# RWKV-7 recurrence and SiLU feed-forward in one kernel: the feed-forward of chunks 0 and 1 worked one chunk at a time, with 256 columns

## The chip, the core and the metric

The kernel runs on one core of one Trainium2 chip. The metric is the time on the device in microseconds, from a launch of the whole program; several runs are taken and the median is given. A profile is one further execution under the hardware profiler; its span reaches from the first to the last instruction of the program.

## What is computed

Two blocks follow each other. The first is a linear recurrence for 4 batches and 8 heads with head dimension 40 over 768 tokens, in float32:

```
for t in range(S):
    y[t]  = r[t] @ state                      # state: D x D per batch and head
    Sa    = state @ a[t]
    state = state * w[t][None, :] - outer(Sa, b[t]) + outer(v[t], k[t])
```

Its output, as 3072 tokens of 8 x 40 = 320 features, goes through a feed-forward block:

```
h = x @ w_in                    # 320 -> 2048
g = h * (1 / (1 + exp(-h)))     # SiLU
out = g @ w_out                 # 2048 -> 320
```

The weights w_in and w_out arrive as float64. The kernel sees them as pairs of 32-bit words and turns them into float32 itself.

## The kernel before

**Chunks and units.** The 768 tokens are cut into 12 chunks of 64 (`NN` = 12). In every chunk there are two units (`NM` = 2), each of two batches. Within a chunk the recurrence is written with matrices: token-by-token products, a triangular system, and a carried state. `pre(u)` prepares a unit before its turn: `scale` (L251 to L262) scans the decays w into running products W on VectorE (L253), takes their reciprocals (L255, VectorE), scales a and kb on GpSimd (L256, L258) and keeps a check on ScalarE (L261, L262); `scores` multiplies b with a on TensorE (`pm`, L231), masks on VectorE (L239) and sends the result to DRAM (`md`, L274). It also asks for the next unit's w (L219), which goes into the one tile `w` that all units from chunk 2 on share. `inverse` then inverts the triangular blocks of two chunks at once, row by row on VectorE (L310, L316), in 15 rows for chunks 0 to 3 and 31 rows from chunk 4 on; `merge` joins the blocks on TensorE (L357, L371, L380 for the 16-row form, L407 and L424 for both).

**The chain.** `chain(u, xs)` is what one unit does in its turn: `keys` (transposes, L473), `right` (L231, L483, L495), `solve` (`pu` L517, `pw` L535), `read` (`pl` L571, masked into `vl` at L579), `write` (`pgy`, L593 and L603; the state Gbd is updated by L616 and L620, and the outputs `yx` of L625 are stored to `xs` in DRAM by L631), and `turn` (L555), which transposes the state for the next chunk. A chunk needs the state that the one before left, so the chains follow one another.

**The feed-forward.** `moe(c, xs)` serves two chunks together: 512 token columns. `fetch` reads `xs` back as `xt` (L646, L648). Then come 16 steps: four `first` (each 256 hidden features: six matmuls `ph`, L658 and L663, of 512 columns; a sigmoid on ScalarE, L666, and the product on VectorE, L667, into `gts`), four `second` (each 128 tokens: eight accumulating matmuls `po`, L674, of 320 columns), and the same again for the other half of the hidden features, where the four `second` add up both halves and store to `out`. The three PSUM banks of `moe_bank` are shared by `ph` and `po`. `in_order` ties every feed-forward matmul behind the one before.

**The weights.** `load_weights(n)` and `weights(n)` bring in 40 pieces, 20 for each half of the hidden features: ten of w_in, then ten of w_out. A piece takes five VectorE instructions (L164, L165, L173, L175, L176) and three on ScalarE (L166 to L168). Raw pieces lie in rooms: up to piece `NG` = 24 four of five lie in a tile that shares its place with `gts`, and pieces from 24 on use the three places `room`, `mi` and `tmp` in rotation. The pieces are asked for five ahead at first, three ahead later.

**Order.** `weave` mixes lists of steps by their relative places. A scheduler then puts the instructions of each engine into one fixed order, and may move a later step forward where it finds the engine free; every engine works off its order strictly. The DMAs go through SyncE's queue in the same manner (some early ones through ScalarE's). The lists for chunks 0 to 3 before the change:

```
weave(steps, convert[6:19])                       # chunk 0's chain
weave(steps[0:4], convert[19:21])                 # chunk 1's chain
weave(steps[4:], convert[21:26], prepare(2))
fetch, queue = moe(0, xs); fetch()
weave(queue[0:12], prepare(3) + convert[26:] + invert(3))
```

From then on the remaining feed-forward steps form a queue, of which chunks 2 and 3 take none by name, and every later chunk takes eight (`now`); what is left at the end is run last.

Of the kernel before, what the change touches and what calls it, by code (L numbers as in the profile page):

```python
# [9 lines left out]
F32 = mybir.dt.float32  # L10
I32 = mybir.dt.int32
U32 = mybir.dt.uint32
AF = mybir.ActivationFunctionType
ALU = mybir.AluOpType
# [18 lines left out]
def weave(*lists):  # L33

    at = [(i + 0.5) / len(x) for x in lists for i in range(len(x))]
    steps = [s for x in lists for s in x]
    for i in sorted(range(len(steps)), key=lambda i: at[i]):
        steps[i]()
# [3 lines left out]
def kernel(  # L42
# [15 lines left out]
    nc = tc.nc  # L58
    NM, NN = aT.shape[0] // 2, aT.shape[1]
# [15 lines left out]
    def moe_bank(name):  # L75
        return ps.tile([128, 512], F32, name=name, tag="moe", bufs=3)
# [52 lines left out]
    for half in range(2):  # L129
# [5 lines left out]
                pieces.append((wl_f[:, c // 2 : c // 2 + WS], [(64 * n, 64 * n + 64, odd[:, n]) for n in range(2)]))  # L135
        for c in range(NF * DM // 2 * half, NF * DM // 2 * (half + 1), WS):
            pieces.append((wo_f[:, c : c + WS], [(0, 128, w_out[:, 2 * c : 2 * (c + WS)])]))
    NW, NG = len(pieces), 24
    rooms = {}

    def load_weights(n, queue=nc.sync):

        if n == 0:
            rooms["gts"] = sb.tile([128, 4, 4 * WS], I32, name="room4", tag="gts")
        if n < NG and n % 5 < 4:
            rooms[n] = rooms["gts"][:, n % 5]
        else:
            tag = "room" if n < NG else ("room", "mi", "tmp")[n % 3]
            rooms[n] = sb.tile([128, 4 * WS], I32, name="room", tag=tag)
        for lo, hi, src in pieces[n][1]:  # L150
            raw = rooms[n][lo:hi, 0 : 2 * WS]
            queue.dma_start(raw.rearrange("p (i x) -> p i x", x=256) if len(src.shape) == 3 else raw, src)
# [46 lines left out]
    def load(u):  # L199
        u.a = sb.tile([128, Q, C], F32, name="a", bufs=4)  # L200
        u.kb = sb.tile([128, Q, 2, C], F32, name="kb", bufs=6)
        B2 = slice(2 * u.m, 2 * u.m + 2)

        def part(n, x):
            for be in range(2):
                nc.sync.dma_start(
                    u.kb[:, P * be : P * be + P, n], x[2 * u.m + be, u.n].rearrange("p (q t) -> p q t", q=P)
                )

        nc.sync.dma_start(  # L210
            u.a.rearrange("p (b q) t -> p b (q t)", b=2), aT[B2, u.n].rearrange("b p c -> p b c")
        )
        part(1, bT)
        part(0, kT)
# [247 lines left out]
    def chain(u, xs):  # L462
# [13 lines left out]
        def right():  # L476
            u.sk = sb.tile([128, 2, P, C], F32, name="sk", bufs=2)
            between(u, 0, u.sk)
            pr = [bank("pr") for _ in range(2)]

            for p in range(P if u.n > 0 else 0):
                for be in range(2):
                    nc.tensor.matmul(  # L483
                        pr[be][C * be : C * be + C, p * 80 : p * 80 + 80],
                        lhsT=u.a[:, P * be + p, :],
                        rhs=gbd[:, P * be + p],
                        start=p == 0,
                        stop=False,
                        skip_group_check=True,
                    )  # L490
            for p in range(P):
                for j in range(2):
                    for be in range(2):
                        R = slice(C * be, C * be + C)
                        nc.tensor.matmul(  # L495
                            pr[be][R, p * 80 + j * D : p * 80 + j * D + D],
                            lhsT=u.sk[R, j, p, :],
                            rhs=u.v2[R, 2 * p + j, :],
                            start=u.n == 0 and p == 0 and j == 0,
                            stop=True,  # L500
                            skip_group_check=True,
                        )
            for be in range(2):
                R = slice(C * be, C * be + C)
                nc.scalar.copy(
                    out=rhs[R, :, :, 0:D],
                    in_=pr[be][R, 0 : H * D].rearrange("p (q j d) -> p q j d", q=P, j=2),
                )
# [127 lines left out]
        return [keys, right, solve, read, write] + ([] if last else [turn])  # L636


    def moe(c, xs):
        T = 4 * NM * C  # L640
        box = {}
        ots = [None] * (T // 128)

        def fetch():
            xt = box["xt"] = sb.tile([128, 3, T], F32, name="xt")
            nc.sync.dma_start(xt[:, 0:2], xs[0:256].rearrange("(k r) t -> r k t", k=2))  # L646
            for n in range(2):
                nc.sync.dma_start(xt[64 * n : 64 * n + 64, 2], xs[256:DM])  # L648

        def first(i):  # L650
            if i % (NF // 4) == 0:
                box["gts"] = sb.tile([128, NF // 2, T], F32, name="gts")
            xt = box["xt"]
            ph = [moe_bank("ph") for _ in range(2)]
            for n in range(2):
                for k in range(2):
                    at = (2 * i + n) * 128
                    in_order(nc.tensor.matmul(  # L658
                        ph[n], lhsT=wi_s[:, k, at : at + 128], rhs=xt[:, k, :], start=k == 0, stop=False
                    ))  # L660
            for n in range(2):
                R = slice(64 * n, 64 * n + 64)
                in_order(nc.tensor.matmul(ph[n], lhsT=wl_s[R, i, :], rhs=xt[R, 2, :], start=False, stop=True))  # L663
            for n in range(2):
                sg = sb.tile([128, T], F32, name="sg", bufs=2)
                nc.scalar.activation(out=sg, in_=ph[n], func=AF.Sigmoid)  # L666
                nc.vector.tensor_tensor(  # L667
                    out=box["gts"][:, (2 * i + n) % (NF // 2), :], in0=ph[n], in1=sg, op=ALU.mult
                )

        def second(half, b):
            po = moe_bank("po")
            for f in range(NF // 2):
                in_order(nc.tensor.matmul(  # L674
                    po[:, 0:DM],
                    lhsT=box["gts"][:, f, b * 128 : b * 128 + 128],
                    rhs=wo_s[:, NF // 2 * half + f, :],
                    start=f == 0,
                    stop=f == NF // 2 - 1,
                ))  # L680
            if half == 0:
                ots[b] = sb.tile([128, DM], F32, name=f"ot{b}")
                nc.scalar.copy(out=ots[b], in_=po[:, 0:DM])
                return
            ot = ots[b]
            nc.vector.tensor_tensor(out=ot, in0=po[:, 0:DM], in1=ot, op=ALU.add)
            n, m = 2 * c + b // NM, b % NM
            for be in range(2):
                at = (2 * m + be) * S + C * n
                nc.sync.dma_start(out[at : at + C, :], ot[C * be : C * be + C, :])  # L690

        steps = []
        for half in range(2):
            steps += [partial(first, NF // 4 * half + i) for i in range(NF // 4)]
            steps += [partial(second, half, b) for b in range(T // 128)]
        return fetch, steps
# [58 lines left out]
    with tc.issue_after(mark["row"]):  # L755
        for u in units[2]:
            load(u)
        run(steps[16:])
        steps = [x for pair in zip(*[x[2:] for x in chains[0]]) for x in pair]
        steps[4:4] = late.pop(0)  # L760
        weave(steps, convert[6:19])
        for u in units[1]:
            load_rv(u)
        for u in units[3]:
            load(u)
        steps = [x for pair in zip(*[chain(u, xs) for u in units[1]]) for x in pair]
        weave(steps[0:4], convert[19:21])
        weave(steps[4:], convert[21:26], prepare(2))
    fetch, queue = moe(0, xs)
    fetch()  # L770
    with tc.issue_after(mark["turn"]):
        weave(queue[0:12], prepare(3) + convert[26:] + invert(3))
    del queue[0:12]
    for n in range(2, NN):
        for u in units[n]:
            load_rv(u)
        for u in units[n + 2] if n + 2 < NN else []:
            load(u)
        if n % 2 == 0:
            xs = dr.tile([DM, 4 * NM * C], F32, name="xs", bufs=2)  # L780
        steps = [x for pair in zip(*[chain(u, xs) for u in units[n]]) for x in pair]
        steps[4:4] = late.pop(n, [])
        now = 8 if n > 3 else 0
        weave(steps[0:4], queue[0 : now // 4])
        weave(steps[4:], queue[now // 4 : now], prepare(n + 2) + invert(n + 2))
        del queue[0:now]
        if n % 2 == 1:
            fetch, more = moe(n // 2, xs)
            fetch()
            queue += more  # L790
    run(queue)
# [155 lines left out]
```

## Time and profile before

| what | value |
|---|---|
| median of 6 runs | 971.38 us |
| lowest and highest | 966.94 and 979.99 us |
| profiled execution, its own time | 970.75 us |
| its span | 969.0 us |
| mean granted TensorE clock | 0.902 |
| busy: PE, PEld, DVE, ACT, POOL | 837.6, 582.5, 531.4, 289.1, 97.5 us |

PE is TensorE's matmuls and PEld its weight loads, DVE is VectorE, ACT ScalarE, POOL GpSimd, SP SyncE. The profiled execution is 1.75 us longer than its span; this lies before the first and after the last instruction. A float32 matmul shows as two records, and the records of matmuls overlap, so a mean duration is longer than the time by which a record advances the engine. In the page's slices a digit is tenths of the slice that the engine was busy, and in the row PEclk tenths of the full TensorE clock. In a timeline each line gives the start, the duration, the engine, the line of the kernel, the operation with its output and inputs, the shapes, how many instructions were merged, and in brackets how long the engine had been idle before it and what it had waited for.

### The profile page before, as it was taken

Reading aid. Unit: us, or ns where it says so; the run is one execution under the profiler, and the core shown is the slowest. Engines: PE = TensorE matmul, PEld = TensorE weight load, DVE = VectorE, ACT = ScalarE, POOL = GpSimd, SP = SyncE. Lnnn points to the kernel's source line nnn. Section 1 sums busy time; section 2 is a strip of 40 time slices with the busy share of each in tenths; the row PEclk is TensorE's granted clock in tenths of the full one; section 3 lists DMA queues with packets and bytes.
Section 4 is the critical chain, followed back from the end, with each engine's and each line's share of the span. In section 5 each row is a group of like instructions: output and inputs, shape, how many; then the busy total and the mean of one; then the engine's idle time right before and its main releaser. Section 6 shows DMA issues by size and latency. Waiting matters only on the chain.

```text
span 969.0 us, 26311 instructions
## 1 busy us (share of the span) xinstructions
PE 837.6 (86%) x11490; PEld 582.5 (60%) x11490; DVE 531.4 (55%) x1062; ACT 289.1 (30%) x644; POOL 97.5 (10%) x98
## 2 busy tenths in 40 slices
PE   0508889699889948999989999989999899999996
PEld 0408778253678823786745876537875568756544
DVE  8964687696116499136895167991558813031111
ACT  2335462352233212235212433213332033210110
POOL 6210011110011101002010011200020000000000
PEclk9855576799789769999999999999999999999998
DMA  9594454543034460355623354413533223002001
GB/s 231 117 226 126 125 140 101 129 113 84 16 92 105 93 150 11 77 129 121 140 63 76 82 141 106 111 32 87 126 91 104 70 49 73 2 15 60 0 1 30
DMA packets 235066, 88.30 MB, mean 91 GB/s; under 512 B 198592, under 2 KB 225728, under 8 KB 234944
## 3 DMA queue, kind: packets, MB, share of 16 engines
q1 hardware_dynamic: 225488, 83.14, 35.7%
q10 hardware_dynamic: 9456, 3.41, 1.7%
q8 instruction: 92, 1.51, 0.6%
q14 instruction: 30, 0.25, 0.1%
HBM read 69.21 MB, written 17.30 MB: 89 GB/s over the span
## 4 chain that ended last, share of the span: by engine, by line
PE 41%; DVE 19%; issue 2%; DMA 2%; SPq 1%; POOL 1%; ACT 0%; POOLq 0%; DVEq 0%
PE po L674 12%; PE ph L658 8%; DVE tmp L310 5%; DVE XI L316 5%; PE pl L571 4%; PE ph L663 2%; DVE gts L667 2%; PE pm L231 2%; PE pgy L603 2%; PE pt L473 2%; PE pu L517 2%; PE pr L495 2%; PE po L424 1%; PE pq L407 1%; DVE w L255 1%
## 5 line engine op out<-in xcount | busy, mean ns | idle before, releaser
L658 PE MATMUL ph<-xt,wi_s 128*128 128x512 f32 x384 | 192.0, 635 | 38.6 <-DMA xt<-xs 19.1
L674 PE MATMUL po<-wo_s,gts 128*128 128x320 f32 x768 | 222.6, 443 | 0.1
L674 PEld LDWEIGHTS po<-wo_s,gts 128*128 128x128 f32 x768 | 143.4, 192 | 61.7 <-issue 4.2
L658 PEld LDWEIGHTS ph<-xt,wi_s 128*128 128x128 f32 x384 | 70.3, 196 | 133.2 <-issue 67.6
L667 DVE TENSOR_TENSOR gts<-ph,sg 128x512 f32<-128x512 f32 x96 | 63.6, 684 | 105.8 <-ACT sg L666 105.7
L666 ACT ACTIVATE sg<-ph 128x512 f32<-128x512 f32 x96 | 52.6, 595 | 223.3 <-PE ph L663 223.2
L310 DVE TENSOR_TENSOR tmp<-XI,mi 128x2 f32<-128x2 f32 (+35 forms) x154 | 76.1, 494 | 5.7 <-DMA mi<-md 1.9
L231 PE MATMUL pm<-a,kb 64*64 64x64 f32 x1536 | 49.4, 241 | 34.0 <-POOL kb L258 19.5
L258 POOL TENSOR_TENSOR kb<-kb,w 128x512 f32<-128x512 f32 x42 | 51.2, 1240 | 269.2 <-DVE w L255 197.5
L316 DVE TENSOR_REDUCE XI<-tmp 128x2 f32<-128x2 f32 (+35 forms) x154 | 71.7, 466 | 3.8
L239 DVE TENSOR_TENSOR sk<-pm,ms 128x256 f32<-128x256 f32 x48 | 18.1, 418 | 97.8 <-PE pm L231 97.8
L255 DVE RECIPROCAL w<-W 128x512 f32<-128x512 f32 x21 | 70.3, 3347 | 0.6
L231 PEld LDWEIGHTS pm<-a,kb 64*64 64x64 f32 x1536 | 40.1, 149 | 45.6 <-POOL kb L258 36.4
L579 DVE TENSOR_TENSOR vl<-pl,ml 128x512 f32<-128x512 f32 x48 | 30.9, 685 | 55.5 <-PE pl L571 55.5
L571 PE MATMUL pl<-r,vut 64*128 64x64 f32 x768 | 58.8, 310 | 0.1
L571 PEld LDWEIGHTS pl<-r,vut 64*128 64x128 f32 x768 | 56.9, 223 | 2.6 <-issue 1.4
L663 PE MATMUL ph<-xt,wl_s 64*128 64x512 f32 x192 | 57.8, 644 | 0.0
L256 POOL TENSOR_TENSOR a<-a,W 128x512 f32<-128x512 f32 x24 | 28.8, 1199 | 275.1 <-DMA a<-in_aT 197.0
L564 ACT COPY GT<-pt 40x512 f32<-40x512 f32 x44 | 25.5, 581 | 79.5 <-PE pt L555 78.8
L603 PE MATMUL pgy<-vl,kt 128*64 128x104 f32 (+1 forms) x768 | 43.4, 273 | 0.0
L239 DVE TENSOR_TENSOR sb<-pm,ms 128x256 f32<-128x256 f32 x48 | 18.2, 412 | 40.4 <-PE pm L231 40.3
L603 PEld LDWEIGHTS pgy<-vl,kt 128*64 128x64 f32 x768 | 38.8, 151 | 1.6
(106 smaller groups left out, 998.9 us busy)
## 6 DMA issues: line engine op xcount, KB each, us to landing
a<-in_aT SPq DMA_DIRECT2D x24, 256.0 KB
kb<-in_bT SPq DMA_DIRECT2D x48, 128.0 KB
kb<-in_kT SPq DMA_DIRECT2D x48, 128.0 KB
vut<-in_vT SPq DMA_DIRECT2D x48, 128.0 KB
r<-in_rT SPq DMA_DIRECT2D x24, 256.0 KB
w<-in_wT SPq DMA_DIRECT2D x40, 128.0 KB
room<-in_w_out SPq DMA_DIRECT2D x20, 256.0 KB
v<-in_v SPq DMA_DIRECT2D x48, 80.0 KB
```

Source lines behind the costliest of these rows:

```text
L231: nc.tensor.matmul(pm[j][C * be : C * be + C, p * C : p * C + C], lhsT=u.kb[J, q, n, :], rhs=u.a[J, q, :], start=True, stop=True,)
L255: nc.vector.reciprocal(R, u.W[:, :, 1 : C + 1])
L258: nc.gpsimd.tensor_tensor(out=u.kb[:, :, n], in0=u.kb[:, :, n], in1=R, op=ALU.mult)
L310: nc.vector.tensor_tensor(out=part, in0=X[:, :, t + 1 : N, t + 1 : N], in1=M[:, :, t, t + 1 : N].unsqueeze(2).to_broadcast([128, I, n, n]) ...
L316: last = nc.vector.tensor_reduce(out=X[:, :, t + 1 : N, t], in_=part, axis=AX.X, op=ALU.add)
L571: nc.tensor.matmul(pl[j][:, q * C : q * C + C], lhsT=u.vut[J, q].rearrange("p n t -> p (n t)"), rhs=u.r[J, q, :], start=True, stop=True,)
L603: nc.tensor.matmul(pgy[be][J, p * N + last * D : p * N + N], lhsT=u.kt[:, P * be + p, J], rhs=u.vl[:, P * be + p, j, last * D :], start=u. ...
L658: in_order(nc.tensor.matmul(ph[n], lhsT=wi_s[:, k, at : at + 128], rhs=xt[:, k, :], start=k == 0, stop=False))
L663: in_order(nc.tensor.matmul(ph[n], lhsT=wl_s[R, i, :], rhs=xt[R, 2, :], start=False, stop=True))
L666: nc.scalar.activation(out=sg, in_=ph[n], func=AF.Sigmoid)
L667: nc.vector.tensor_tensor(out=box["gts"][:, (2 * i + n) % (NF // 2), :], in0=ph[n], in1=sg, op=ALU.mult)
L674: in_order(nc.tensor.matmul(po[:, 0:DM], lhsT=box["gts"][:, f, b * 128 : b * 128 + 128], rhs=wo_s[:, NF // 2 * half + f, :], start=f == 0, ...
```

## The change

The feed-forward of chunks 0 and 1 is no longer worked as one set of 512 columns. `moe` takes the first chunk and a count, so that a set can be of one chunk (256 columns, 12 steps: four `first` and two `second` for each half) or of two (as before). Chunk 0's set is fetched before chunk 1's chain, and its first five steps (four `first`, one `second`) are woven into that chain, behind the last matmul of its `right`. Chunk 1's set follows. The conversions of the weights are spread anew: two more in chunk 0's chain, three in place of two and ten in place of five in chunk 1's chain, the rest behind it. `gts` becomes two tiles with two places each: for a single chunk one tile holds a half's eight products, for two chunks a half lies across two tiles. The rooms that share its place follow, and only pieces below 20 use them. Chunk 2's list takes five steps of the queue by name and chunk 3's six.

```diff
-    NW, NG = len(pieces), 24
+    NW, NG = len(pieces), 20
 ...
-            rooms["gts"] = sb.tile([128, 4, 4 * WS], I32, name="room4", tag="gts")
+            rooms["gts"] = [sb.tile([128, 2, 4 * WS], I32, name="room2", tag="gts", bufs=2) for _ in range(2)]
         if n < NG and n % 5 < 4:
-            rooms[n] = rooms["gts"][:, n % 5]
+            rooms[n] = rooms["gts"][n % 5 // 2][:, n % 5 % 2]
 ...
-                        nc.tensor.matmul(
+                        mark["right"] = nc.tensor.matmul(
                             pr[be][R, p * 80 + j * D : p * 80 + j * D + D],
 ...
-    def moe(c, xs):
-        T = 4 * NM * C
+    def moe(n0, count, xs):
+        W = 2 * NM * C
+        T = W * count
+
+        NG = NF // 2 // count
+        at = slice(W * (n0 % 2), W * (n0 % 2) + T)
 ...
-            nc.sync.dma_start(xt[:, 0:2], xs[0:256].rearrange("(k r) t -> r k t", k=2))
+            nc.sync.dma_start(xt[:, 0:2], xs[0:256, at].rearrange("(k r) t -> r k t", k=2))
 ...
+        def place(f):
+            f %= NF // 2
+            return box["gts"][f // NG][:, f % NG]
 ...
-                box["gts"] = sb.tile([128, NF // 2, T], F32, name="gts")
+                box["gts"] = [sb.tile([128, NG, T], F32, name="gts", bufs=2) for _ in range(count)]
 ...
-            ph = [moe_bank("ph") for _ in range(2)]
+            ph = [moe_bank("ph")[:, 0:T] for _ in range(2)]
 ...
-        weave(steps, convert[6:19])
+        weave(steps, convert[6:21])
 ...
+        fetch, queue = moe(0, 1, xs)
+        fetch()
         steps = [x for pair in zip(*[chain(u, xs) for u in units[1]]) for x in pair]
-        weave(steps[0:4], convert[19:21])
-        weave(steps[4:], convert[21:26], prepare(2))
-    fetch, queue = moe(0, xs)
+        weave(steps[0:4], convert[21:24])
+        issued["last"] = mark["right"].ins
+        weave(steps[4:], queue[0:5], convert[24:34], prepare(2))
+        del queue[0:5]
+    fetch, more = moe(1, 1, xs)
     fetch()
+    queue += more
     with tc.issue_after(mark["turn"]):
-        weave(queue[0:12], prepare(3) + convert[26:] + invert(3))
-    del queue[0:12]
+        weave(queue[0:5], prepare(3) + convert[34:] + invert(3))
+    del queue[0:5]
 ...
-        now = 8 if n > 3 else 0
+        now = 8 if n > 3 else n + 3
 ...
-            fetch, more = moe(n // 2, xs)
+            fetch, more = moe(n - 1, 2, xs)
```

More of the change, by code (lines that the diff above doesn't have):

```diff
@@ L645, in fetch @@
             xt = box["xt"] = sb.tile([128, 3, T], F32, name="xt")
-            nc.sync.dma_start(xt[:, 0:2], xs[0:256].rearrange("(k r) t -> r k t", k=2))
+            nc.sync.dma_start(xt[:, 0:2], xs[0:256, at].rearrange("(k r) t -> r k t", k=2))
             for n in range(2):
-                nc.sync.dma_start(xt[64 * n : 64 * n + 64, 2], xs[256:DM])
+                nc.sync.dma_start(xt[64 * n : 64 * n + 64, 2], xs[256:DM, at])
+        def place(f):
+            f %= NF // 2
+            return box["gts"][f // NG][:, f % NG]
         def first(i):
             if i % (NF // 4) == 0:
-                box["gts"] = sb.tile([128, NF // 2, T], F32, name="gts")
+                box["gts"] = [sb.tile([128, NG, T], F32, name="gts", bufs=2) for _ in range(count)]
             xt = box["xt"]
-            ph = [moe_bank("ph") for _ in range(2)]
+            ph = [moe_bank("ph")[:, 0:T] for _ in range(2)]
             for n in range(2):
@@ L667, in first @@
                 nc.vector.tensor_tensor(
-                    out=box["gts"][:, (2 * i + n) % (NF // 2), :], in0=ph[n], in1=sg, op=ALU.mult
+                    out=place(2 * i + n), in0=ph[n], in1=sg, op=ALU.mult
                 )
@@ L675, in second @@
                     po[:, 0:DM],
-                    lhsT=box["gts"][:, f, b * 128 : b * 128 + 128],
+                    lhsT=place(f)[:, b * 128 : b * 128 + 128],
                     rhs=wo_s[:, NF // 2 * half + f, :],
@@ L686, in second @@
             nc.vector.tensor_tensor(out=ot, in0=po[:, 0:DM], in1=ot, op=ALU.add)
-            n, m = 2 * c + b // NM, b % NM
+            n, m = n0 + b // NM, b % NM
             for be in range(2):
```

## The prediction

> **What bounds the kernel now.** I began with the page's forty slices. PE is nearly full, and its granted clock reaches full speed only after the first third.
>
> ```profile
> PE   0508889699889948999989999989999899999996
> DVE  8964687696116499136895167991558813031111
> ...
> PEclk9855576799789769999999999999999999999998
> ```
>
> Then I cut the span into stages: chunk 1's chain (121.6 to 164.5: from the state update L616 of chunk 0's second unit to the end of chunk 1's, L620), feed-forward 0 (164.5 to 250), the chains of chunks 2 and 3 (250 to 344), the 32-row inversion behind them, chunks 4 to 11, the tail. The columns are PE, PEld, DVE, ACT and POOL busy, then clock and DMA.
>
> ```profile
> 121.60:164.50 42.90, 38.19 (x635) 35.76 (x633) 32.84 (x70) 18.89 (x46) 7.24 (x6) 0.72 0.50 128
> 164.50:250.00 85.50, 72.63 (x416) 36.61 (x416) 59.37 (x128) 32.03 (x72) 9.63 (x9) 0.86 0.40 99
> 250.00:344.00 94.00, 84.86 (x2041) 72.03 (x2040) 34.45 (x69) 27.33 (x62) 10.40 (x10) 0.82 0.35 82
> ...
> 433.00:867.00 434.00, 417.93 (x5777) 285.06 (x5775) 250.67 (x476) 126.83 (x271) 35.62 (x30) 1.00 0.35 84
> ```
>
> From 433 on PE is the bound, full and at clock 1.00: later time is gained only by reaching it earlier. The page's chain of waits goes back only to 326, so what bounds the earlier stages is read from the PE timeline (start, duration, idle before it):
>
> ```profile
> 171.36 1.13 PE L231 MATMUL pm<-a,kb 64*64 64x64 f32 x32 [1.99 <-POOL kb L258]
> 178.24 5.76 PE L658 MATMUL ph<-xt,wi_s 128*128 128x512 f32 x8 [5.74 <-DMA xt<-xs]
> ...
> 199.13 3.47 PE L658 MATMUL ph<-xt,wi_s 128*128 128x512 f32 x4 [2.29 <-DVE gts L667]
> ...
> 229.99 3.61 PE L658 MATMUL ph<-xt,wi_s 128*128 128x512 f32 x4 [2.34 <-DVE gts L667]
> ```
>
> Chunk 1's chain ends, PE has nothing until xt is fetched (5.74 us), starts cold (5.76 for what takes 3.70 warm), and waits on silu products behind weight conversions on VectorE. The inversion for chunks 2 and 3 starts only at 219.8, behind the last conversion.
>
> **Durations at full clock**, from the tail:
>
> ```profile
> 934.61 3.70 PE L658 MATMUL ph<-xt,wi_s 128*128 128x512 f32 x8
> 938.24 1.13 PE L663 MATMUL ph<-xt,wl_s 64*128 64x512 f32 x4
> ...
> 943.99 17.49 PE L674 MATMUL po<-wo_s,gts 128*128 128x320 f32 x64
> ```
>
> The next `first` starts at 939.30, so one costs 4.69 us at 512 columns, 2.35 at 256 if columns alone count; 17.43 us for 64 `po` records is 0.272 a record, 4.35 a `second`. A matmul is two records.
>
> **Do 256 columns hide their weight load?** Twice the 96 `ph` records of 512 columns become 192, each with its own load. The `po` records, loading 128x128 as well, take 0.85 ns a column at 320 (0.272/320), and 16 transposes of 128 columns (L473, one follows the other from 408.95 to 410.84) take 1.9 us, 0.93 ns a column; 512 columns take 0.89. So nothing shows as load down to 128: extra 0. The Trainium skill ("TensorE: Matmul & The Clock Gate") speaks against the change: its section "Why this matters for your kernels" wants fewer than 512 columns padded up, and "Part 3: Packing small matmuls" lets a load overlap running matmuls only where its row group differs, which full 128-row loads don't; its figure for a load, columns over 1.2, gives 107 ns. By the rule 96 more loads cost 10.3 us, by the rows 0. I take the rows; from the transposes a load is at most 119 ns, 11.4 us in all, my upper end.
>
> **Stage one, chunk 1's chain.** The compiled order of the changed kernel puts three `first` before the end of the chain and the fourth behind its last `pgy`: 3 x 2.35 = 7.05 us more PE work. Five more conversions move here (five VectorE instructions of about 0.2 to 0.34 us net, 1.4 together, so 7), one of the two reciprocals of 3.35 moves out, and six half products come in at 0.37 (the nearest row: L239 from PSUM, 128x256, mean 412 ns less overlap): VectorE 32.8 + 7 - 3.35 + 2.2 = 38.7 of 42.9. It fits. PE would not fit at the old clock, but 140 to 150 shows PE busy 10.00 at clock 0.50: chains of 64x64 matmuls leave the clock low, whereas 402 to 433, chains mixed with feed-forward, stand at 1.00. The page's rule ("Part 1: The HAM clock gate": some 3.4 us of busy PE give full clock) would have the chain warm already, and the sum +7. By the row, 38.19 us at 0.72 are 27.5 at full clock; plus 7.05 is 34.5, at an expected 0.9 about 38.4, with the same 4.7 idle 43.1. I take **0**, bounds -6 and +9. On SP the new fetch of xs stands behind chunk 2's `v` load and a chunk-3 `a` (130.06 in before): I expect its issue near 132 and landing 4.3 later (173.95 to 178.24 before), about when PE arrives; whatever is late stalls unit 1's `pu` behind it.
>
> **Stage two, to the merge matmuls of chunk 2 (L371).** Now: 85.5. After, PE holds before L371 five `first` of chunk 0, seven of chunk 1 (12 x 2.35 = 28.2), 48 `po` (48 x 0.545 = 26.1), and turns, scores and L357 of about 7: 61.3. The 5.74 wait goes, since chunk 0's work covers chunk 1's fetch. What is late next: in the new order the last scores of chunk 3 (`pm`) stand between two `first`, and need a reciprocal whose operand w is loaded once the last one's readers finish. From a reciprocal's end to the next scan took 5.5 and 7.2 us (134.9 to 140.40, 148.64 to 155.84). The preceding reciprocal ends some 9 us in; 9 + 6.4 + 1.3 (scans) + 0.7 + 3.35 + 1.24 (POOL) = 22, and PE is there at 16: wait **6**. Products behind reciprocal and conversions cost a further **4** (2.3 each in before, over shorter steps). 61.3 + 10 = 71.5. VectorE, read off its order: 8 opening pairs of conversions (L164, L165) at 0.4, 9.5 closing triples at 1.0, three reciprocals at 3.3, five scans at 0.6, six score products at 0.37, `yx` 0.8 and ten silu products at 0.37, or 32 us, where before it was busy 43.5 of the 55.3 us from 164.5 to 219.8. With its waits for PE, then 12.4 of rows (219.8 to 232.2) with products between and the transfers that follow, the inverse is there about 62 us in: it hides under PE, but barely. Saving **14**, bounds 6 and 19.
>
> **Stage three, chains 2 and 3.** Feed-forward fillers fall from 24 `po` (13.1) to a partial `first` and 16 `po` (10.7). Chains wait on other engines too: **-1**, bounds -3 and +3.
>
> **Later.** Both kernels have finished the first two chunks' feed-forward by chunk 3's end; remaining work is equal. The queue holds 19 steps for 20, so one `second` (4.35) moves from the tail into chunk 7 and stays ahead. Where PE bounds, that is nothing. At 777.44 PE waited for the inverted blocks: there 3.6 us less filler means idling. **+3**, bounds 0 and +5. The other edits cost nothing: the two halves of gts hold the same bytes, 20 instead of 24 weight pieces use it, at start both kernels convert about equally before chunk 1.
>
> **Sum.** 970.75 (span 969.0 and 1.75 around it, unchanged) + 0 - 14 - 1 + 3 = **959**, against a median of 971.38.
>
> **Rivals.**
> *Weight loads show*: up to +11.4 us on the forecast, 970, no change. For: the rule. Against: the row at 320.
> *The clock stays low in chunk 1*: the three `first` add 7 us, 9 with their own cold columns: 968. For: the gaps between them. Against: 402 to 433.
> *More gain*: chain shortened by 6, stage two by 19: 948.
> *ScalarE blocked by weight transfers, slower*: pieces 20 to 29 now arrive within chunk 1's chain through three rooms, and ScalarE's L168 waits for each transfer with sigmoid, `vl` and `vut` copies queued behind, for which PE and the chain wait. Before, such waits took 2.81 and 7.61 us, harmlessly. Ten pieces at 2.81 give +28: 987. Above 1.2 us a piece the gain is gone. Against: the transfers' issue to their use spans about 3 us or more in the order.
> That nothing moves is excluded by the order.
>
> **Numbers.** Forecast 0.54, low clock 0.16, loads 0.07, more gain 0.10, blocked 0.13. A measurement of this kernel tells about 1% (961.7) from no change. Of the forecast 0.45 lies below it, plus 0.10 and 0.03 of low clock: faster 0.58; slower 0.14, the blocked case and a little; the same 0.28. The range takes the bounds and most of the rivals: 945 to 976; the likeliest case alone spans 950 to 966.
>
> **To check after.** Right if the stretch from L620 of chunk 0 to that of chunk 1 stays near 43 us at clock near 0.9, no xt wait of 5 us, L371 about 72 us behind, 256-column records spaced 227 ns, a wait of about 6 for kb before `pm`, and from chunk 4 the old pace. Wrong if ScalarE shows long waits on room transfers inside chunk 1's chain, if records are spaced well over 227, or if the gain is lost again at the inversions.

## The result, and the profile after

The changed kernel takes **963.1 us** (median of 16 runs, 956.86 to 970.16) against 971.19 for the kernel before in runs on the same chips: ratio **0.9918, 95% interval 0.9894 to 0.9941**. It is faster by 0.8%: the interval leaves out 1, though the gain is smaller than the 1% that the prediction took as what can be told from no change. The profiled execution took 964.7 us, span 962.9, where 959 was forecast.

First the slices of the page of the changed kernel, the same three rows as before.

```profile
PE   0407799799989848999989999979999999999996
...
DVE  8955689982106499145894267981649813031111
...
PEclk9755699899659669999999999999999999999999
```

The clock of the slices around chunk 1's chain has risen, but slices 11 and 12 (240 to 290 us) are now at 0.6 and 0.5. A gain early and a loss in the chains of chunks 2 and 3: the stages put numbers on both. A stage ends at the last L620 of a chain or at the first L371 of chunk 2; columns as before (PE, PEld, DVE, ACT, POOL busy, then clock and DMA). The changed kernel:

```profile
122.80:160.10 37.30, 36.01 (x638) 29.73 (x637) 32.34 (x87) 24.63 (x62) 3.53 (x3) 0.95 0.63 169
160.10:237.40 77.30, 66.76 (x496) 43.93 (x493) 58.45 (x121) 26.24 (x70) 13.23 (x12) 0.93 0.41 99
237.40:339.60 102.20, 91.39 (x2035) 77.71 (x2034) 34.41 (x70) 28.12 (x64) 10.40 (x10) 0.72 0.30 72
...
431.70:859.00 427.30, 413.14 (x5622) 280.05 (x5622) 245.99 (x463) 125.86 (x269) 35.46 (x30) 0.99 0.35 83
```

The kernel before, chunk 1's chain between the same points:

```profile
124.00:164.50 40.50, 36.51 (x603) 34.24 (x601) 30.58 (x63) 17.72 (x44) 7.24 (x6) 0.71 0.51 129
```

| part of the span | before | after | difference | forecast |
|---|---|---|---|---|
| up to the end of chunk 0's chain | 124.0 | 122.8 | -1.2 | 0 |
| stage one, chunk 1's chain | 40.5 | 37.3 | -3.2 | 0 |
| stage two, to L371 of chunk 2 | 85.5 | 77.3 | -8.2 | -14 |
| stage three, chains 2 and 3 | 94.0 | 102.2 | **+8.2** | -1 |
| everything later | 625.0 | 623.3 | -1.7 | +3 |
| span | 969.0 | 962.9 | -6.1 | -12 |

By the merge matmuls of chunk 2 the changed kernel is 12.6 us ahead, almost what was forecast. The chains of chunks 2 and 3 then give 8.2 back. Multiplying PE's busy time by the clock gives an estimate of the work at full clock: 84.86 x 0.82 = 69.6 before, 91.39 x 0.72 = 65.8 after. So the stage does *less* work in more time; the clock takes the difference. Each stage is read from one profile. Three more profiles, of the two kernels with fillers and of the one with halves further down, have the same VectorE order in chunk 1's chain as the changed kernel and took 38.1, 38.5 and 39.3 us for its 37.3, so a difference of 2 us in this stage says little.

The PE timeline of the changed kernel shows the steps that the prediction asked for (start, duration, idle before and its releaser).

```profile
134.09 1.99 PE L666 MATMUL ph<-xt,wi_s 128*128 128x256 f32 x8
...
138.75 1.99 PE L666 MATMUL ph<-xt,wi_s 128*128 128x256 f32 x8
...
181.85 1.13 PE L231 MATMUL pm<-a,kb 64*64 64x64 f32 x32 [4.51 <-POOL kb L258]
183.92 2.07 PE L666 MATMUL ph<-xt,wi_s 128*128 128x256 f32 x4 [0.94 <-DVE gts L675]
...
193.67 1.13 PE L666 MATMUL ph<-xt,wi_s 128*128 128x256 f32 x4 [2.50 <-DVE gts L675]
...
318.96 1.13 PE L231 MATMUL pm<-a,kb 64*64 64x64 f32 x32 [4.04 <-POOL kb L258]
```

The first `first` starts inside chunk 1's chain without waiting for xt (5.74 us before). The new wait for kb before `pm` is there with 4.51 us, and waits for silu products of 0.94 and 2.50. The last line is one that the prediction had not asked for: the same wait in chunk 3's chain, 1.88 us before, is 4.04 now.

### The profile page after: what moved, and what is told of

The parts are those of the page before. It is cut to its first block, busy times and chain, and to the rows that moved or that the text cites. A ratio compares the mean times of both kernels' runs of the same rounds, so it can differ in the third digit from the quotient of the medians.

```text
span 962.9 us, 26553 instructions
## 1 busy us (share of the span) xinstructions
PE 833.8 (87%) x11586; PEld 586.1 (61%) x11586; DVE 531.8 (55%) x1078; ACT 290.4 (30%) x660; POOL 97.1 (10%) x98
## 3 DMA queue, kind: packets, MB, share of 16 engines
q10 hardware_dynamic: 9456, 3.41, 1.7%
## 4 chain that ended last, share of the span: by engine, by line
PE 57%; DVE 30%; issue 4%; DMA 4%; ACT 2%; POOL 1%; SPq 1%; ACTq 0%; POOLq 0%; DVEq 0%
PE po L682 15%; PE ph L666 10%; DVE tmp L310 6%; DVE XI L316 6%; PE pl L571 4%; PE ph L671 4%; DVE w L255 3%; PE pq L407 3%; PE pgy L603 3%; PE pu L517 2%; PE po L424 2%; PE pm L231 2%; DVE W L253 2%; DVE gts L675 2%; PE pt L473 2%
## 5 line engine op out<-in xcount | busy, mean ns | idle before, releaser
L682 PE MATMUL po<-wo_s,gts 128*128 128x320 f32 x768 | 225.8, 446 | 0.6 <-DVE gts L675 0.4
L666 PE MATMUL ph<-xt,wi_s 128*128 128x512 f32 (+1 forms) x448 | 194.6, 570 | 31.1 <-DVE gts L675 15.7
L666 PEld LDWEIGHTS ph<-xt,wi_s 128*128 128x128 f32 x448 | 82.8, 199 | 116.2 <-issue 57.7
L675 DVE TENSOR_TENSOR gts<-ph,sg 128x512 f32<-128x512 f32 (+1 forms) x112 | 65.8, 608 | 137.6 <-ACT sg L674 137.5
L674 ACT ACTIVATE sg<-ph 128x512 f32<-128x512 f32 (+1 forms) x112 | 54.9, 534 | 235.2 <-PE ph L671 235.2
L231 PE MATMUL pm<-a,kb 64*64 64x64 f32 x1536 | 48.8, 242 | 39.1 <-POOL kb L258 37.6
L671 PE MATMUL ph<-xt,wl_s 64*128 64x512 f32 (+1 forms) x224 | 63.7, 606 | 0.0
L571 PEld LDWEIGHTS pl<-r,vut 64*128 64x128 f32 x768 | 48.4, 200 | 4.7 <-issue 2.1
L571 PE MATMUL pl<-r,vut 64*128 64x64 f32 x768 | 49.7, 285 | 1.1 <-DVE vl L579 1.1
L671 PEld LDWEIGHTS ph<-xt,wl_s 64*128 64x128 f32 x224 | 19.3, 196 | 35.0 <-issue 33.5
```

The source lines that it names most:

```text
L231: nc.tensor.matmul(pm[j][C * be : C * be + C, p * C : p * C + C], lhsT=u.kb[J, q, n, :], rhs=u.a[J, q, :], start=True, stop=True,)
L571: nc.tensor.matmul(pl[j][:, q * C : q * C + C], lhsT=u.vut[J, q].rearrange("p n t -> p (n t)"), rhs=u.r[J, q, :], start=True, stop=True,)
L666: in_order(nc.tensor.matmul(ph[n], lhsT=wi_s[:, k, at : at + 128], rhs=xt[:, k, :], start=k == 0, stop=False))
L675: nc.vector.tensor_tensor(out=place(2 * i + n), in0=ph[n], in1=sg, op=ALU.mult)
L682: in_order(nc.tensor.matmul(po[:, 0:DM], lhsT=place(f)[:, b * 128 : b * 128 + 128], rhs=wo_s[:, NF // 2 * half + f, :], start=f == 0, stop ...
```

## Experiments: which part of the change gains

The prediction's theory is the cover by feed-forward. The rival is the edit that looks like bookkeeping: the conversions of the weights were cut into other slices, and 20 pieces for 24 go through the gts room. Each part was run alone.

**Conversions alone.** In the kernel before:

```diff
-    NW, NG = len(pieces), 24
+    NW, NG = len(pieces), 20
 ...
-        weave(steps, convert[6:19])
+        weave(steps, convert[6:21])
 ...
-        weave(steps[0:4], convert[19:21])
-        weave(steps[4:], convert[21:26], prepare(2))
+        weave(steps[0:4], convert[21:24])
+        weave(steps[4:], convert[24:34], prepare(2))
 ...
-        weave(queue[0:12], prepare(3) + convert[26:] + invert(3))
+        weave(queue[0:12], prepare(3) + convert[34:] + invert(3))
```

> The kernel before with the conversions alone spread as in the changed kernel (and only pieces below 20 in the rooms that share gts); the feed-forward of chunks 0 and 1 stays one set of 512 columns. Theory A (the gain is chunk 0's feed-forward filling chunk 1's chain and covering the fetch of xt; the conversions only make room for it): the wait of 5 to 6 us for xt and the cold start stay, VectorE reaches the inversion earlier, the stretch from chunk 1's end to L371 falls from 85.5 us to about 81; time 967 to 970. Theory B (the gain is the conversions, which free VectorE before the inversion): that stretch is 77 as in the changed kernel, time 963.

Measured: 0.9896 [0.9863, 0.9929]. A gain as large as the change's comes without one of its 256-column feed-forwards. L371 of chunk 2 is reached at 231.4, 6 us earlier than in the changed kernel.

**The change with the old conversions** (slices 6:19, 19:21, 21:26, 26: put back, all else as changed).

> The changed kernel with the conversions spread as before (0 to 18 by chunk 0's chain, 19 and 20, then five, in chunk 1's). Theory A: chunk 1's chain and the covered fetch stay as in the changed kernel, products wait a few us longer behind conversions, and the inversion starts 5 us later: time 964 to 967. Theory B: back to 971.

Measured: 0.9947 [0.9917, 0.9977]. Feed-forward and its split alone gain half a percent, with an interval that overlaps the changed kernel's.

**The change without feed-forward inside chunk 1's chain.**

```diff
-        issued["last"] = mark["right"].ins
-        weave(steps[4:], queue[0:5], convert[24:34], prepare(2))
-        del queue[0:5]
+        weave(steps[4:], convert[24:34], prepare(2))
 ...
-        weave(queue[0:5], prepare(3) + convert[34:] + invert(3))
-    del queue[0:5]
+        weave(queue[0:10], prepare(3) + convert[34:] + invert(3))
+    del queue[0:10]
```

> The changed kernel with all of chunk 0's feed-forward behind chunk 1's chain instead of its first five steps within it; split, conversions and rooms as changed. Theory A: chunk 1's chain is cold again (clock about 0.7 instead of 0.96) and 3 us longer; the fetch of xt is still covered; 14 us of matmuls move behind the chain, partly into chains 2 and 3, which are warmer: time 966 to 969. Rival (the gain is the split alone: xt fetched early and finer steps; where the five steps stand does not matter): 963.

Measured: 0.9892 [0.9856, 0.9928]. Taking the feed-forward out of chunk 1's chain loses nothing. The two parts do not add up: 0.5% and 1.0% alone, 0.8% together.

The conversions' part has two edits of its own, so they were split too. **Rooms alone** (only the 24 made 20) and **slices alone** (only the four `weave` lines), both in the kernel before:

> The kernel before with one number changed: 20 instead of 24 weight pieces go through the gts room. If the earlier use of the three other rooms is what the conversions' part gains (room theory), ratio about 0.990. If the order on VectorE does it (order theory), the room is nothing: ratio 0.997 to 1.003, chunk 1's chain still 40 us, inversion rows still starting near 219.

> The kernel before with only the four slices of conversions moved ahead (24 pieces through the gts room as before). Order theory: ratio about 0.990 as with both, chunk 1's chain 33 to 35 us, rows starting near 200. Room theory: 0.997 to 1.003.

Measured: rooms alone **1.0103** [1.0046, 1.0161], slower; slices alone **0.9868** [0.9810, 0.9925]. The gain lies in the slices, and the smaller number of rooms is a cost in the kernel before: its profile has stage two at 90.5 us for 85.5 and stage three at 102.5 for 94.0. Why the rooms cost this was not followed further. It is not a cost everywhere. The changed kernel with 24 pieces through the two gts tiles (one number):

> The changed kernel with 24 instead of 20 weight pieces through the two gts tiles, all else equal. e5_rooms lost 1.0% by the smaller number in the kernel before, e6_slices gained 1.3% without it. If the rooms cost that everywhere: ratio 0.980 to 0.986. Rival: with feed-forward in chunk 1's chain the gts tiles are needed for products, those wait for pieces 20 to 23, chunk 1's chain grows by 3 to 6 us, ratio 0.995 to 1.00.

Measured: 0.9937 [0.9906, 0.9968], the same as the changed kernel within the intervals. In its profile chunk 1's chain took 40.3 us for 37.3, which is the rival's direction but little more than the spread of that stage, stage two was 2.0 shorter, and L371 stood at 237.6 for 237.4. So 20 pieces in place of 24 are neither a gain nor a cost that could be told there.

**Why do the slices shorten chunk 1's chain?** They move instructions on VectorE against each other. In the kernel before, VectorE's timeline has chunk 2's first reciprocal between the two masked products `sk` of the chain:

```profile
129.36 0.76 DVE L239 TENSOR_TENSOR sk<-pm,ms 128x256 f32<-128x256 f32 x2 [0.99 <-PE pm L231]
...
131.55 3.35 DVE L255 RECIPROCAL w<-W 128x512 f32<-128x512 f32 x1
134.81 0.69 DVE L239 TENSOR_TENSOR sk<-pm,ms 128x256 f32<-128x256 f32 x2
```

The second unit's `sk` stands behind 3.35 us of reciprocal, and PE has to wait for what follows from it. The clock falls to one half at 138.0, some 0.3 us after that wait has begun (137.75), and stays there until 158.5 (PE timeline and two windows of the kernel before):

```profile
139.44 2.92 PE L517 MATMUL pu<-RHS,XT 64*64 64x40 f32 x29 [1.69 <-ACT RHS L505]
```

```profile
134.64:138.05 3.41, 2.59 (x74) 2.33 (x72) 3.41 (x7) 2.43 (x7) 2.50 (x2) 1.00 0.62 170
138.04:158.52 20.48, 19.08 (x218) 18.49 (x220) 12.43 (x24) 7.83 (x21) 3.52 (x3) 0.50 0.43 105
```

So the 1.69 us did not lower the clock alone: most of them lie behind the fall, and in the 3.41 us ahead of it PE had been busy 2.59. That VectorE's order costs the chain its clock is a theory of its own, tested by moving nothing but the preparation of chunk 2, in the kernel before:

```diff
-        weave(steps[4:], convert[21:26], prepare(2))
+        weave(steps[4:], convert[21:26])
 ...
-        weave(queue[0:12], prepare(3) + convert[26:] + invert(3))
+        weave(queue[0:12], prepare(2) + prepare(3) + convert[26:] + invert(3))
```

> The kernel before with the preparation of chunk 2 (two scans, two reciprocals of 3.35 us, their scores) taken out of chunk 1's chain and put behind it, ahead of chunk 3's; conversions where they were. Reciprocal theory (the gain is the shorter chain, since no reciprocal stands ahead of its products on VectorE): chain 33 to 35 us and 4 to 6 us of span gained, ratio 0.994 to 0.996. Rival (the gain is that VectorE has the conversions behind it before the inversion): chain shorter, but rows start no earlier than 219, nothing left of it at the merge matmuls, ratio 0.998 to 1.004.

Measured: 0.9916 [0.9887, 0.9946], more than expected. VectorE's timeline of this kernel, then PE's at the same `pu`, then the chain as a whole:

```profile
131.69 0.76 DVE L239 TENSOR_TENSOR sk<-pm,ms 128x256 f32<-128x256 f32 x2
...
136.66 3.35 DVE L255 RECIPROCAL w<-W 128x512 f32<-128x512 f32 x1
```

```profile
135.66 1.39 PE L517 MATMUL pu<-RHS,XT 64*64 64x40 f32 x27 [0.33 <-ACT RHS L505]
```

```profile
124.80:151.90 27.10, 22.81 (x564) 20.44 (x561) 24.15 (x58) 17.19 (x42) 3.61 (x3) 1.00 0.62 163
```

The reciprocal now stands behind both `sk`, PE waits 0.33 us for 1.69, the clock stays at 1.00 and the chain takes **27.1 us for 40.5**: 13.4 us gained, where the two reciprocals of 3.35 us, of which one has left the chain, come to 6.7 in all. An estimate from the two windows of the chain (PE busy times clock) says where they lie. PE is idle about as long in both, 4.0 and 4.3 us. The work at full clock is 3.1 us less, 25.9 before (36.51 x 0.71) and 22.8 now. The other 10.6 us (36.51 - 25.9) were time at half clock. The test shows what the preparation costs inside this chain; which of its instructions lets the clock fall was not tried alone. Only a part of it reaches the end, because the preparation now stands in stage two, which grows from 85.5 to 89.6 (and stage three to 99.1). The slices do a good part of the same by their order (in the conversions-alone kernel the reciprocal starts at 135.92, behind both `sk`, and the next at 165.94, behind the chain, which takes 33.1 us). In addition VectorE has less left to convert ahead of the inversion, whose rows start at 199.4 for 219.8 in the slices-alone kernel.

## Experiments: where stage three lost its time

**Which part of it.** The stage is parted at chunk 3's first key transposes (L473). Ahead of them stand the merges of chunks 2 and 3 and chunk 2's chain, behind them chunk 3's chain. The kernel before, then the changed kernel:

```profile
250.00:306.00 56.00, 49.47 (x1418) 41.16 (x1417) 14.83 (x36) 16.00 (x35) 3.40 (x4) 0.82 0.29 71
306.00:344.00 38.00, 35.39 (x624) 30.87 (x624) 19.62 (x34) 11.33 (x28) 7.00 (x6) 0.82 0.42 97
```

```profile
237.40:300.50 63.10, 57.09 (x1419) 47.30 (x1418) 14.87 (x37) 16.69 (x37) 3.40 (x4) 0.68 0.24 58
300.50:339.60 39.10, 34.30 (x616) 30.41 (x616) 19.55 (x34) 11.43 (x28) 7.00 (x6) 0.78 0.41 95
```

| kernel | stage three | ahead of the transposes | behind them |
|---|---|---|---|
| before | 94.0 | 56.0 | 38.0 |
| changed | 102.2 | 63.1 | 39.1 |
| slices alone | 94.9 | 62.8 | 32.1 |
| preparation of chunk 2 moved | 99.1 | 67.0 | 32.1 |
| rooms alone | 102.5 | 63.3 | 39.2 |

Of the 8.2 us, 7.1 are lost ahead of the transposes. By the same estimate as above, the work there is no more (40.6 us at full clock before, 38.8 now), and PE is idle for 6.5 and 6.0 us; the clock makes the difference. It stood at one half from 254.1 to 267.8 and from 278.0 to 284.8 in the kernel before, and from 239.1 to 256.2 and from 263.0 to 286.9 in the changed one, 20.5 and 41.0 us. PE's longest waits in the two merges are 2.03 and 2.58 us before, 1.73 and 2.38 now, so longer waits do not explain it, and no run shows what does. There is one profile of the kernel before, and no other kernel of the table comes near its 56.0.

**Feed-forward held back.** If the chains of chunks 2 and 3 lack cover, give them some: the second half of chunk 1's feed-forward was tied into them.

```diff
-        weave(queue[0:5], prepare(3) + convert[34:] + invert(3))
-    del queue[0:5]
+        weave(queue[0:13], prepare(3) + convert[34:] + invert(3))
+    del queue[0:13]
 ...
-        now = 8 if n > 3 else n + 3
-        weave(steps[0:4], queue[0 : now // 4])
-        weave(steps[4:], queue[now // 4 : now], prepare(n + 2) + invert(n + 2))
+        now = 8 if n > 3 else 3
+        first = 0 if n < 4 else now // 4
+        weave(steps[0:4], queue[0:first])
+        if n < 4:
+            issued["last"] = mark["right"].ins
+        weave(steps[4:], queue[first:now], prepare(n + 2) + invert(n + 2))
```

> The changed kernel with the last six feed-forward steps of chunk 1 (four first, two second, 18 us) tied behind chunk 2's right, so that they stand within the chains of chunks 2 and 3, whose start no longer waits for them. Theory C (of the 14 us forecast for the second stage 8 were made, and chains 2 and 3 gave them back because, short of feed-forward, they run at clock 0.72): the stretch to L371 falls by about 9 us, chains 2 and 3 run at 0.85 or more in no more than 100 us in spite of more work, time 950 to 957. Rival (these chains are bound by their own order and the low clock is only its sign): what is saved before L371 is paid within the chains, time 962 to 968.

Measured: **1.0059** [1.0032, 1.0087], slower. Chunk 3's chain ended at 330.3 for 339.6, and the later part took 642.0 for 623.3. The edit also shortened the queue from chunk 5 on, to 16 steps for 19. With `now = 8 if n > 4 else 5 if n == 4 else 3` the queue is as long as in the changed kernel again:

> As e4_hold (second half of chunk 1's feed-forward held back into the chains of chunks 2 and 3), with chunk 4 taking five steps for eight, so that from chunk 5 the queue is as long as in the changed kernel, 19 steps. Queue theory (e4's loss of 19 us behind chunk 3 came from three steps missing at each inversion): the 9 us that chain 3 ended earlier remain, span near 955, ratio 0.981 to 0.987. Rival (held-back work is simply paid later, wherever): chunk 4's chain longer by what chunk 3's was shorter, ratio 0.99 to 1.00.

Measured: **0.9846** [0.9795, 0.9897], the lowest ratio of the study, though its interval touches those of the slices-alone and the changed kernel. The later part is 625.8. PE's waits for xt in the later part (from the end of chunk 3's chain), first with the short queue, then with the long one (us in total, times, longest):

```profile
PE ph L666 <- DMA xt<-xs: 32.1, 5, 10.2
```

```profile
PE ph L666 <- DMA xt<-xs: 11.2, 1, 11.2
```

So three steps of feed-forward missing at each inversion cost 16 us: PE runs out of work and waits for the next xt five times in place of once. In all it is idle for 48.2 us of the later part, for 35.9 with the long queue. But stage three itself still took 103.1 us: its gain lies ahead of it (L371 at 231.4), and feed-forward in the chains did not raise the clock there (0.74).

**What follows a wait.** Now the smaller part, behind the transposes, where the `pm` of chunk 3's chain waits 4.04 us in the changed kernel. The clock behind it:

```profile
318.80:332.40 13.60, 13.44 (x202) 13.09 (x204) 3.33 (x6) 1.84 (x6) 1.25 (x2) 0.50 0.26 50
```

The slices-alone kernel has the same `pm` with a short wait, and this behind it (PE timeline, then windows):

```profile
315.12 0.69 PE L231 MATMUL pm<-a,kb 64*64 64x64 f32 x32 [0.81 <-POOL kb L258]
```

```profile
315.00:322.00 7.00, 6.85 (x192) 6.62 (x192) 2.98 (x6) 1.79 (x6) 1.21 (x2) 1.00 0.43 79
322.00:329.00 7.00, 7.00 (x141) 5.89 (x139) 5.38 (x16) 1.16 (x2) 0.00 (x0) 1.00 0.39 98
```

The same chain at 1.00 in place of 0.50, and 32.1 us for 39.1. But the length of the wait does not decide it. In the kernel with the preparation of chunk 2 moved the same `pm` waits 2.96 us, and the clock stays at 1.00 behind it (PE timeline, then windows):

```profile
326.98 0.69 PE L231 MATMUL pm<-a,kb 64*64 64x64 f32 x32 [2.96 <-POOL kb L258]
```

```profile
327.00:334.00 7.00, 6.97 (x194) 6.70 (x196) 3.12 (x6) 1.65 (x6) 1.06 (x1) 1.00 0.48 91
334.00:341.00 7.00, 6.25 (x140) 5.61 (x141) 5.38 (x16) 1.16 (x2) 0.00 (x0) 1.00 0.38 87
```

To turn the comparison into a test, the gap was filled in the changed kernel. A helper `fill(n, behind)` issues n matmuls of 128x320 on constants into a bank that nothing reads:

```diff
-                        nc.tensor.matmul(
+                        pw_last = nc.tensor.matmul(
 ...
+            if (u.n, u.m) == (3, 0):
+                fill(7, pw_last.ins)
```

> The changed kernel with seven filler matmuls (128x320, products of constants that nothing reads, 14 records, 3.8 us at full clock) behind the pw of chunk 3's first unit, where PE waits 4.04 us for kb before pm and then runs at half clock to about 335. Gap theory (an idle PE of some 2 us costs the clock for the 10 to 20 us behind it): clock stays at 1.00 through the rest of chain 3, chain 3 ends 7 to 9 us earlier, ratio 0.982 to 0.986. Rival (the clock there follows something else, the kind of matmul or the chip's state): still 0.5 behind the filler, ratio 0.990 to 0.996 as for the changed kernel alone.

Measured: 0.998 [0.9949, 1.0010]. PE's timeline with the filler (line numbers are shifted by the helper), then the clock:

```profile
300.30 4.04 PE L193 MATMUL junk<-wo_s,ident 128*128 128x320 f32 x14
...
305.36 0.69 PE L240 MATMUL pm<-a,kb 64*64 64x64 f32 x32 [0.48 <-POOL kb L267]
```

```profile
307.00:314.00 7.00, 7.00 (x85) 5.09 (x84) 0.00 (x0) 1.84 (x5) 0.00 (x0) 1.00 0.67 133
314.00:321.00 7.00, 7.00 (x78) 5.95 (x77) 2.69 (x7) 0.43 (x1) 0.00 (x0) 1.00 0.29 75
321.00:328.00 7.00, 7.00 (x138) 5.89 (x137) 6.33 (x29) 0.66 (x2) 0.00 (x0) 1.00 0.50 108
```

With the gap filled the clock stays at 1.00 to the end of the chain, as the gap theory says, and the chain ended at 334.8 for 339.6. That the gap alone had lowered it is not shown, since the 2.96 us above did not. The time does not follow: with the seven added instructions the scheduler laid out the rest anew. 32 `po` and 28 `ph` records stand in chunk 3's chain for 16 and none in the changed kernel, the next inversion's rows started at 319.2, inside the chain, and the later part took 639.1 us for 623.3. As a test of the time it is inconclusive. With fillers in the merges of chunks 2 and 3 as well (`fill(4, last.ins)` between L357 and L371):

> As e9_fill_pm, and four more fillers (2.2 us) in each of the merges of chunks 2 and 3, between the products of L357 and those of L371, where PE waits 1.7 and 2.4 us and the clock then stands at 0.5 for some 13 and 20 us. Gap theory: the stretch from L371 to the end of chain 3 falls from 102 us to 80 to 87, span near 943 to 950, ratio 0.970 to 0.978. Rival: the fillers cost their 8 us or nothing, stretch 98 to 110, ratio 0.99 or more.

Measured: 1.0109 [1.0082, 1.0136]. The clock stands at 1.00 from 264 to 305 and from 312 to 342, and the kernel is slower all the same, with the order moved as in the run before. The expectation was missed, and a higher clock is no gain by itself.

**The price of 256 columns.** All the changed kernel's later `first` were written as two halves too. "The rule" is the prediction's, from the Trainium skill ("TensorE: Matmul & The Clock Gate", "LDWEIGHTS (loading the stationary operand)"): 107 ns for a load of 128 columns.

```diff
-                        ph[n], lhsT=wi_s[:, k, at : at + 128], rhs=xt[:, k, :], start=k == 0, stop=False
 ...
+                    for x in range(0, T, 256):
 ...
+                            ph[n][:, x : x + 256], lhsT=wi_s[:, k, at : at + 128], rhs=xt[:, k, x : x + 256],
+                            start=k == 0 and x == 0, stop=False, skip_group_check=True
 ...
```

> The changed kernel with every first of the five 512-column pairs (chunks 2 to 11) written as two halves of 256 columns too: 480 more ph records, each with its own weight load, in stretches where PE is the bound at full clock. By the rows (a load of 128 columns hides beside the matmul ahead of it) nothing is added: eight wi_s records of the tail in 1.8 us, time as the changed kernel's, ratio 0.990 to 0.996. By the rule (a load of 107 ns stands alone) 480 x 0.107 = 51 us more, ratio 1.04 to 1.05.

Measured: six runs from 960.83 to 981.59 us, too far apart for a ratio; but even the slowest is only 1.01 of the kernel before (972.26), where the rule had 1.04 to 1.05. The tail, where PE has nothing but feed-forward, gives the price of one step. First the halves, then the changed kernel with 512 columns (both PE timelines):

```profile
940.23 3.72 PE L667 MATMUL ph<-xt,wi_s 128*128 128x256 f32 x16
943.88 1.14 PE L674 MATMUL ph<-xt,wl_s 64*128 64x256 f32 x8
944.95 3.72 PE L667 MATMUL ph<-xt,wi_s 128*128 128x256 f32 x16
```

```profile
923.60 3.70 PE L666 MATMUL ph<-xt,wi_s 128*128 128x512 f32 x8
927.23 1.13 PE L671 MATMUL ph<-xt,wl_s 64*128 64x512 f32 x4
928.29 3.70 PE L666 MATMUL ph<-xt,wi_s 128*128 128x512 f32 x8
```

One `first` from start to start: 944.95 - 940.23 = 4.72 us with 24 records, 928.29 - 923.60 = 4.69 with 12. Twelve loads more cost 0.03 us, 2.5 ns each, where 107 by the rule would have made 1.3 us of it.

## Why the prediction was right, and where it was not

The direction and the range held; the median lies 4 us above the forecast, the profiled run 5.7. The mechanism held in part. The waits and the work of stage two were sized well, but a gain as large comes with the slices of the conversions alone, which the prediction had booked as 7 us more for VectorE, and the cover by feed-forward adds none on top of it that could be told. By its steps:

- **Weight loads cost 0.** Right; the tail above shows 2.5 ns a load. The rule that the prediction weighed against it, 107 ns, is not borne out for these fp32 records.
- **Stage one, 0.** Made -3.2, inside its bounds, but its reasoning failed. The prediction read PE busy 10.00 of 10 us at clock 0.50 as a property of chains of 64x64 matmuls and expected feed-forward to lift it. The run with chunk 2's preparation moved has the same chain, with no feed-forward, at clock 1.00. What lifts the clock there is the place of the preparation on VectorE; in the changed kernel the new slices move its reciprocals too (to 132.8, behind both `sk`, and to 165.6, behind the chain). VectorE was forecast 38.7 us busy in this stretch, and was 34.59 (120.4 to 160.1).
- **Stage two, -14.** Made -8.2. The waits were sized well: 4.5 us for kb (6 forecast), 3.9 for silu products (4), none for xt. PE's work was also right, at full clock: 61.3 forecast, and 66.76 x 0.93 = 62.1 measured, an estimate. The terms left out are the clock of 0.93, 4.7 us by the same estimate, and two small waits (1.4 for `yx`, 0.5 for `ot`).
- **Stage three, -1.** Made +8.2: **the step that failed.** "Chains wait on other engines too" counted fillers and took the clock as it was, 0.82. It was 0.72. Of the loss, 7.1 us lie ahead of chunk 3's transposes, where the clock went from 0.82 to 0.68 with no longer waits at the merges; why stays open. The wait for kb before chunk 3's `pm`, 4.04 us for 1.88, stands in the part that lost 1.1. The prediction had named a gain lost again at the inversions as a sign of being wrong, and here it came true at the merges that end one.
- **Later, +3.** Made -1.7. One queue step less was no cost here; that a few steps matter was right, since three less cost 16 us.
- **Rival, ScalarE blocked.** Not seen: L168 waited twice for a room inside chunk 1's chain, 4.6 us together, but PE's longest wait there is 1.09 us, and that for VectorE.

That the sum came so near is in part luck. Stages two and three were 15.0 us worse than forecast, and the start, stage one and the later part 9.1 us better.

## What to carry to other kernels

When a change has a main idea and a bookkeeping part, run each alone: here the order of the weight conversions made a gain as large as the whole change's, and the feed-forward, for which they were moved, half a percent alone and none that could be told on top of it. Price a long VectorE instruction not by its 3.35 us but by what is queued behind it, and look at the clock before the idle time: moving the preparation out of a chain gave 13.4 us while PE was idle for as long as before. And when an edit moves a queue, keep its length at the points where later work falls back on it: three steps were worth 16 us.

## What the runs showed of the hardware

**The clock changes at set moments.** Read in windows of 1 us, it changed in the kernel before at 124.4, 127.8, 138.0, 158.5, 165.4, 182.4, 199.5 and 202.9: these are 1, 3, 6, 2, 5, 5 and 1 times 3.41 us apart. In seven traces read in this way from 100 to 350 us (the kernel before, the changed one, rooms alone, slices alone, preparation moved, and the two with fillers) every change lies on such a grid to about 0.1 us, each trace with its own offset. So a half clock lasts a whole number of these stretches, however short the wait before it.

**A single wait does not tell whether it falls.** In four of these traces (all but slices alone and the two with fillers), from 117 to 350 us, every fall follows a stretch with idle time in it, PE busy 3.35 of 3.41 us or less, and every rise a stretch that PE filled. Neither is enough. In the rooms-alone kernel the clock fell behind a stretch whose one long wait was 0.61 us, and later it stayed at one half for 27 us in which PE was never idle:

```profile
127.24:130.66 3.42, 2.81 (x51) 2.56 (x48) 3.42 (x3) 1.40 (x4) 0.19 (x1) 1.00 0.64 189
130.66:134.07 3.41, 2.89 (x60) 2.74 (x59) 3.06 (x7) 2.83 (x8) 2.31 (x2) 0.50 0.78 215
...
277.43:304.74 27.31, 27.31 (x424) 23.57 (x424) 4.40 (x9) 6.59 (x16) 0.00 (x0) 0.50 0.22 53
```

In the kernel with the preparation moved it stayed at 1.00 behind the wait of 2.96 us shown above. The Trainium skill ("TensorE: Matmul & The Clock Gate", section "HAM oscillation — how this bites in real kernels") warns of idle gaps above some 3.4 us; here the clock fell with no wait above 0.61 us in one trace and did not fall behind one of 2.96 in another. What decides, and why one half clock lasts 3.4 us (199.5 to 202.9 in the kernel before) and another 27, stays open: no run here isolates it, and the length decides what such a fall is worth. It is also not tried what a second `w` tile would do, which might take away the wait for kb.
